# Loading a 256-element vector as one row and turning it on TensorE, in a recurrence and mixture-of-experts kernel

## The chip, the cores and the metric

The kernel runs on one core of a Trainium2 chip. The metric is the device time of one execution, in microseconds (us). It was run three times before the change; the median of these three runs is the time that counts, and lower is better.

## The reference, cut to what matters

Two stages follow each other. The first is a gated recurrence over a sequence, for 4 sequences of 5056 steps and 256 channels:

```python
sig = 1.0 / (1.0 + np.exp(-f_logit))
f = lower_bound[None, None, :] + (1.0 - lower_bound[None, None, :]) * sig
i = 1.0 - f
for t in range(S):
    h = f[:, t] * h + i[:, t] * x[:, t]
    y[:, t] = h
```

The second takes y as 20224 tokens and is a soft mixture of experts: `logits = x @ phi` for 32 slots, a softmax over the tokens that gathers them into slots, two matmuls for each of 8 experts with a ReLU between them, and a softmax over the slots that spreads the result back to the tokens.

`lower_bound` is a vector of 256 floats, 1 KB. Since f = 1 - (1 - lower_bound) * sigmoid(-f_logit), the kernel needs of it only `omlb` = 1 - lower_bound and `nomlb` = lower_bound - 1. Both are needed with channels on partitions: partition p holds the channels 2p and 2p + 1.

## The kernel before, in words

**Units.** The sequence is cut into groups of 512 tokens, and a unit is one group of one of the 4 sequences: 40 units. `load` (L195) issues the loads of `f_logit` (tile `f_t`) and `x` (tile `x_t`) on SyncE's queue (SP). The first six units are loaded one by one, 512 KB for each tensor (L216); the long middle part goes in transfers of 1 MB (L202). Three pairs of units fit the load buffers, so a later load waits for a buffer to come free.

**What a unit passes through.** ScalarE (ACT) computes sigmoid(-f) into `s_t` (`gate`, L226). GpSimd (POOL) multiplies it with x into `u_t` (`enter`, L237; VectorE does it for unit 0, L233). TensorE (PE) turns both from tokens on partitions to channels on partitions (`s_to_channels` and `u_to_channels`, L252 and L258, into the PSUM tiles `sp` and `up`). ACT makes the decay `a` = 1 + `nomlb` * s out of `sp` (`decay`, L286 and L293). VectorE (DVE) runs the recurrence as a scan (L304). PE turns the result back (`to_tokens`, L317, into the tile `hp`, which has the only PSUM buffer with the tag `tp`), DVE or ACT copies it out (`keep_tokens`, L334), and the matmuls of the second stage follow (`logits` L348, `slots` L398). At L174 PE runs matmuls that only add zero, as fillers. The expert weights are loaded on POOL's queue late in the first stage (L130, L140); then come the expert matmuls, and last the output blocks: matmul at L704 and L754, scaling at L694, L759 and L765, and stores on SP's queue.

**The order of the work** is written out by hand (`tc.manual_schedule()`); every engine executes its instructions in the order in which they are issued in the program, and waits on the semaphores of what it needs.

**The start, which the change touches.** `make_identity` builds `ident_f` on POOL. L75 loads `lower_bound` on ACT's queue into `lb`, and L79 loads phi on POOL's queue. Then DVE sets some constants. After the `load` calls of the first six units (L454), `lb_constants` (L103) computes `omlb` (L104) and `nomlb` (L105) on DVE. `gate(0)`, `enter(0)`, `s_to_channels(0)` and `decay(0)` come next: the first reader of `nomlb` is ACT's decay at L293. `phi_constants` (L107) follows on POOL: it scales phi by `omlb` (L109). `omlb` is read once more, much later (L598, L599).

The lines that count:

```python
lb = consts.tile([P, DC], F32, name="lb")
nc.scalar.dma_start(out=lb, in_=lower_bound.rearrange("(p o) -> p o", o=DC))
...
for n in range(SINGLE):
    load(n, 1)
lb_constants()
gate(0, 1)
enter(0)
s_to_channels(0)
```

Of the kernel before, what the change touches and what calls it, by code (L numbers as in the profile page):

```python
# [9 lines left out]
F32 = mybir.dt.float32  # L10
# [8 lines left out]
def kernel(  # L19
# [10 lines left out]
    nc = tc.nc  # L30
    B, S, D = x.shape
# [4 lines left out]
    P = 128  # L36
    DC = D // P
    FC = F // P
    R = 4
# [27 lines left out]
    consts = ctx.enter_context(tc.tile_pool(name="consts", bufs=1))  # L67
    ident_f = consts.tile([P, P], F32, name="ident_f")
# [2 lines left out]

    rep = consts.tile([P, B, NS], F32, name="rep")

    lb = consts.tile([P, DC], F32, name="lb")
    nc.scalar.dma_start(out=lb, in_=lower_bound.rearrange("(p o) -> p o", o=DC))  # L75
    omlb = consts.tile([P, DC], F32, name="omlb")
    nomlb = consts.tile([P, DC], F32, name="nomlb")
    phi_f = consts.tile([P, DC, NS], F32, name="phi_f")
# [22 lines left out]
        nc.vector.memset(parity[ds(b * NS, NS), ds(b % 2, 1)], 1.0)  # L101

    def lb_constants():  # L103
        nc.vector.tensor_scalar(omlb, lb, -1.0, 1.0, ALU.mult, ALU.add)  # L104
        nc.vector.tensor_scalar(nomlb, lb, 1.0, -1.0, ALU.mult, ALU.add)  # L105

# [49 lines left out]
    with tc.tile_pool(name="sp2", bufs=3) as sp2, \  # L156
# [297 lines left out]
# [5 lines that stand above are left out]
# [368 lines left out]
```

## Time and profile before

| | |
|---|---|
| three runs | 200.14, 200.80, 200.83 us; median 200.8 us |
| span of the profiled execution | 198.1 us; its own device time is not listed, so what lies around the span is 2.0 to 2.7 us by these runs |
| busy share of the span | PE 77%, DVE 72%, ACT 70%, PE's weight loads 56%, POOL 52% |
| moved by DMA | 70.77 MB, mean 357 GB/s |
| SP's DMA queue (q1) | 11520 packets, 62.00 MB |
| ACT's DMA queue (q10) | 288 packets, 0.13 MB |
| load of `lb` | 1 KB, issued at 0.72 us, landed 4.3 us later |
| `omlb`, `nomlb` on DVE | 169 ns, 164 ns |

The profile is that of one execution. Times in it count from the start of the span. "Busy" is the time in which an engine executed instructions. The chain of work that ended last is followed back from the last instruction: at each step to what released it, or to the instruction before it on its engine. In the table of stretches, the columns are the stretch and its length, then for PE, PE's weight loads (PEld), DVE, ACT and POOL the busy time with the number of instructions, then the TensorE clock that was granted (1.00 is full speed), the mean busy share of the 16 DMA engines, and the rate at which they moved data. A DMA queue's line gives the number of packets, the MB, and the time of its packets as a share of the 16 engines' time.

### The profile page before, as it was taken

Reading aid. Unit: us, or ns where it says so; the run is one execution under the profiler, and the core shown is the slowest. Engines: PE = TensorE matmul, PEld = TensorE weight load, DVE = VectorE, ACT = ScalarE, POOL = GpSimd, SP = SyncE. Lnnn points to the kernel's source line nnn. Section 1 sums busy time; section 2 is a strip of 40 time slices with the busy share of each in tenths; the row PEclk is TensorE's granted clock in tenths of the full one; section 3 lists DMA queues with packets and bytes.
Section 4 is the critical chain, followed back from the end, with each engine's and each line's share of the span. In section 5 each row is a group of like instructions: output and inputs, shape, how many; then the busy total and the mean of one; then the engine's idle time right before and its main releaser. Section 6 shows DMA issues by size and latency. Waiting matters only on the chain.

```text
span 198.1 us, 3497 instructions
## 1 busy us (share of the span) xinstructions
PE 153.3 (77%) x1330; PEld 110.4 (56%) x1330; DVE 143.3 (72%) x164; ACT 138.7 (70%) x195; POOL 103.0 (52%) x78
## 2 busy tenths in 40 slices
PE   0587599987999989898997978999989999950000
PEld 0366478776776768676695856568953543310000
DVE  1669869999699999999989999523268878840000
ACT  2688677899889999999897595622069889980000
POOL 2489578774998688884969969290030000000000
PEclk9999759997999999999999999999995555555555
DMA  5999999999999999999999999999639999999995
GB/s 177 418 420 419 427 429 429 427 427 357 378 424 424 408 337 420 432 411 307 407 420 392 241 215 214 213 212 211 110 110 419 430 421 427 450 443 424 424 424 218
DMA packets 14448, 70.77 MB, mean 357 GB/s; under 512 B 1744, under 2 KB 3024, under 8 KB 10464
## 3 DMA queue, kind: packets, MB, share of 16 engines
q1 hardware_dynamic: 11520, 62.00, 75.5%
q0 software_dynamic: 2624, 8.42, 21.3%
q8 instruction: 10, 0.16, 0.3%
q10 hardware_dynamic: 288, 0.13, 0.2%
q14 instruction: 6, 0.05, 0.1%
HBM read 58.23 MB, written 20.71 MB: 399 GB/s over the span
## 4 chain that ended last, share of the span: by engine, by line
PE 32%; DMA 30%; DVE 18%; POOL 6%; issue 3%; ACT 1%; ACTq 0%; SPq 0%; POOLq 0%
DMA x_t<-in_x_dram 15%; DVE h L304 13%; PE op L754 12%; DMA w_t<-in_moe_w_dram 8%; DMA w_sb<-in_moe_w_dram 7%; POOL u_t L237 5%; PE hp L317 4%; PE up L258 4%; PE sp L252 3%; DVE ht L334 3%; PE op L704 2%; PE slot_ps L174 2%; PE lg L348 1%; PE slot_ps L398 1%; DVE ob L694 1%
## 5 line engine op out<-in xcount | busy, mean ns | idle before, releaser
L237 POOL TENSOR_TENSOR u_t<-s_t,x_t 128x1024 bf16<-128x1024 bf16 (+1 forms) x39 | 82.5, 2128 | 23.3 <-ACT s_t L226 13.9
L304 DVE TENSOR_TENSOR_SCAN h<-a,h,up 128x512 bf16<-128x512 f32 (+1 forms) x72 | 86.9, 1252 | 4.7 <-PE up L258 2.5
L226 ACT ACTIVATE s_t<-f_t 128x2048 bf16<-128x2048 f32 (+2 forms) x23 | 38.3, 1668 | 5.8 <-DMA f_t<-in_f_logit_dram 4.5
L317 PE MATMUL hp<-ident_f,h 128*128 128x128 f32 (+1 forms) x160 | 29.5, 309 | 7.3 <-DVE ht L334 6.0
L317 PEld LDWEIGHTS hp<-ident_f,h 128*128 128x128 f32 (+1 forms) x160 | 23.1, 208 | 15.3 <-DVE ht L334 9.6
L252 PE MATMUL sp<-ident_f,s_t 128*128 128x128 f32 x144 | 22.6, 303 | 10.1 <-ACT s_t L226 7.8
L286 ACT ACTIVATE a<-sp,nomlb 128x1024 f32<-128x1024 bf16 x24 | 25.4, 1114 | 0.8 <-PE sp L252 0.6
L252 PEld LDWEIGHTS sp<-ident_f,s_t 128*128 128x128 f32 x144 | 18.6, 158 | 11.8 <-issue 6.0
L754 PE MATMUL op<-slot_bd,etall 64*128 64x512 bf16 x62 | 24.4, 600 | 0.1
L765 ACT ACTIVATE oc<-op,rrow 128x256 f32<-128x256 f32 x60 | 22.8, 490 | 1.4 <-PE op L754 0.9
L759 DVE TENSOR_TENSOR oc<-op,rrow 128x1024 f32<-128x1024 f32 x16 | 19.3, 1223 | 4.6 <-PE op L754 4.5
L293 ACT ACTIVATE a<-sp,nomlb 128x512 f32<-128x512 bf16 (+2 forms) x22 | 17.9, 859 | 4.8 <-PE sp L252 4.4
L258 PE MATMUL up<-ident_f,u_t 64*128 64x64 f32 x192 | 17.6, 229 | 2.0 <-POOL u_t L237 1.9
L174 PE MATMUL slot_ps<-rep,ident 128*128 128x256 bf16 x122 | 17.7, 281 | 0.0
L258 PEld LDWEIGHTS up<-ident_f,u_t 64*128 64x128 f32 x192 | 13.9, 138 | 5.9 <-POOL u_t L237 2.4
L754 PEld LDWEIGHTS <-etall 64*128 64x128 bf16 x62 | 9.0, 153 | 14.2 <-issue 11.6
L334 ACT COPY ht<-hp 128x512 f32<-128x512 f32 (+1 forms) x18 | 10.4, 580 | 8.0 <-PE hp L317 7.9
L334 DVE COPY ht<-hp 128x512 f32<-128x512 f32 (+1 forms) x22 | 14.7, 668 | 0.8 <-PE hp L317 0.8
L174 PEld LDWEIGHTS <-ident 128*128 128x128 bf16 x126 | 11.4, 102 | 3.4 <-issue 1.3
L304 DVE TENSOR_TENSOR_SCAN h<-a,up 128x512 bf16<-128x512 f32 x8 | 9.3, 1209 | 2.5 <-ACT a L293 1.8
L252 PE MATMUL up<-ident_f,u_t 128*128 128x128 f32 x48 | 9.8, 337 | 0.6 <-POOL u_t L237 0.6
L348 PE MATMUL lg<-h,phi 128*32 128x512 bf16 (+1 forms) x80 | 10.0, 411 | 0.0
(105 smaller groups left out, 147.8 us busy)
## 6 DMA issues: line engine op xcount, KB each, us to landing
f_t<-in_f_logit_dram SPq DMA_DIRECT2D x12, 1024.0 KB, 12.3
x_t<-in_x_dram SPq DMA_DIRECT2D x12, 1024.0 KB, 11.4
out_dram<-oc SPq DMA_DIRECT2D x6, 2048.0 KB, 13.1
w_sb<-in_moe_w_dram POOLq DMA_DIRECT2D x14, 512.0 KB, 10.3
f_t<-in_f_logit_dram SPq DMA_DIRECT2D x12, 512.0 KB, 8.6
x_t<-in_x_dram SPq DMA_DIRECT2D x12, 512.0 KB, 9.4
out_dram<-oc SPq DMA_DIRECT2D x4, 896.0 KB, 6.1
out_dram<-ob SPq DMA_DIRECT2D x1, 2048.0 KB, 8.9
```

Source lines behind the costliest of these rows:

```text
L174: nc.tensor.matmul(slot_bank[:, 1, ds(0, rhs.shape[1])], ident, rhs, start=first and i < 2, stop=False, skip_group_check=True)
L226: nc.scalar.activation(s_t, f_t, ACT.Sigmoid, scale=-1.0)
L237: nc.gpsimd.tensor_tensor(uts[n][:, :r], s_t[:, :r], x_t[:, :r], ALU.mult)
L252: nc.tensor.transpose(ps[:, :, r], t[:, r], ident_f)
L258: nc.tensor.transpose(v[:, :, r], t(r)[k].bitcast(F32), ident_f[k, k])
L286: nc.scalar.activation(a, sp[:, :, :, :, o], ACT.Identity, scale=nomlb[:, ds(o, 1)], bias=1.0)
L304: nc.vector.tensor_tensor_scan(h[:, :T, o], decays[n // 2, o][:, n % 2, :T], up[:, :T, o], hs[number(g - 1, b)][:, ds(used(g - 1) - 1, 1), ...
L317: nc.tensor.transpose(hp[:n_p, r], hw[:, :n_p, r], ident_f)
L334: copy(hts[g][:n_p, b].rearrange("p r d -> p (r d)").bitcast(F32), hps.pop(n)[:n_p].rearrange("p r c -> p (r c)"))
L754: nc.tensor.matmul(op[:, i_r].rearrange("p u d -> p (u d)"), ew[:, :, r + i_r], slot_bd[ds(j * 2 * NS, 2 * NS)].rearrange("s u d -> s (u d)"),
L759: nc.vector.tensor_tensor(ob[:, :, ds(r, k)].rearrange("p u r d -> p r u d"), op[:, ds(0, k)], scale[:, ds(r, k)].unsqueeze(3).broadcast_t ...
L765: nc.scalar.activation(ob[:, u, r + i_r], op[:, i_r, u], ACT.Copy, scale=scale[:, r + i_r, ds(u, 1)])
```

## The change

The vector is loaded as one contiguous row of 256 floats on partition 0. In `lb_constants`, two TensorE transposes with a 1x1 identity then turn the even and the odd channels of that row into two columns on 128 partitions, in a PSUM tile that takes the buffer with the tag `tp`. `omlb` and `nomlb` are computed from this PSUM tile.

```diff
-    lb = consts.tile([P, DC], F32, name="lb")
-    nc.scalar.dma_start(out=lb, in_=lower_bound.rearrange("(p o) -> p o", o=DC))
+    lb_row = consts.tile([1, D], F32, name="lb_row")
+    nc.scalar.dma_start(out=lb_row, in_=lower_bound.unsqueeze(0))
...
     def lb_constants():
+        row = lb_row.rearrange("u (p o) -> u p o", o=DC)
+        lb_ps = ptp.tile([P, R, P], F32, name="lb_ps", tag="tp")
+        lb = lb_ps[:, 0, ds(0, DC)]
+        for o in range(DC):
+            nc.tensor.transpose(lb_ps[:, 0, ds(o, 1)], row[:, :, o], ident_f[ds(0, 1), ds(0, 1)])
         nc.vector.tensor_scalar(omlb, lb, -1.0, 1.0, ALU.mult, ALU.add)
         nc.vector.tensor_scalar(nomlb, lb, 1.0, -1.0, ALU.mult, ALU.add)
```

## The prediction

> **What bounds the kernel now.** I read the page first, then the chain of work that ended last in order of time, then the first microseconds: the timeline, the table of stretches, and the DMA queues stretch by stretch.
>
> From the page: the span, the slices of 4.95 us, and the chain's shares.
>
> ```profile
> span 198.1 us, 3497 instructions
> ...
> PEclk9999759997999999999999999999995555555555
> DMA  5999999999999999999999999999639999999995
> GB/s 177 418 420 419 427 429 429 427 427 357 378 424 424 408 337 420 432 411 307 407 420 392 241 215 214 213 212 211 110 110 419 430 421 427 450 443 424 424 424 218
> ...
> PE 32%; DMA 30%; DVE 18%; POOL 6%; issue 3%; ACT 1%; ACTq 0%; SPq 0%; POOLq 0%
> ```
>
> No engine bounds the whole; the bound changes from stage to stage. From the second to the ninth slice (5 to 45 us) the loads run flat out at 418 to 429 GB/s; after that the rate moves with the engines. So the first 40 us are paced by the loads. The chain, with start, length and what it is, says the same:
>
> ```profile
> 0.72 0.38 SPq L216
> 1.10 0.06 issue
> 1.16 4.89 DMA x_t<-in_x_dram
> 6.05 0.02 issue
> 6.06 10.30 DMA x_t<-in_x_dram
> ...
> 21.26 13.88 DMA x_t<-in_x_dram
> ...
> 39.96 0.04 issue
> 40.00 0.46 PE up L258 x4
> ```
>
> The chain starts with unit 0's x (issued 1.16, landed 6.05) and stays on x transfers, with two POOL multiplies between, until 35.14; POOL multiplies lead to 40 us, and PE and DVE follow. Whatever shifts the load stream shifts all of this.
>
> The load of `lb` itself is not on the chain. From the timeline (start, length, engine, line):
>
> ```profile
> 4.85 1.06 ACT L226 ACTIVATE s_t<-f_t 128x1024 bf16<-128x1024 f32 x1 [2.41 <-DMA f_t<-in_f_logit_dram]
> 5.02 0.17 DVE L104 TENSOR_SCALAR omlb<-lb 128x2 f32<-128x2 f32 x1 [2.99 <-DMA lb<-in_lower_bound_dram]
> 5.10 0.16 DVE L105 TENSOR_SCALAR nomlb<-lb 128x2 f32<-128x2 f32 x1
> 7.17 0.69 ACT L293 ACTIVATE a<-sp,nomlb 128x512 f32<-128x512 bf16 x1 [1.27 <-PE sp L252]
> ```
>
> `nomlb` is ready at 5.26; its first reader starts at 7.17, and waits for PE. As a latency, `lb` has 1.9 us to spare. But the first slice moves only 177 GB/s. The table of stretches of half a microsecond shows where:
>
> ```profile
> 2.00:2.50 0.50, 0.00 (x0) 0.00 (x0) 0.04 (x2) 0.44 (x1) 0.31 (x1) 1.00 0.26 90
> 3.00:3.50 0.50, 0.00 (x0) 0.00 (x0) 0.00 (x0) 0.00 (x0) 0.00 (x0) 1.00 0.83 213
> 4.00:4.50 0.50, 0.00 (x0) 0.00 (x0) 0.00 (x0) 0.00 (x0) 0.00 (x0) 1.00 1.05 402
> 4.50:5.00 0.50, 0.00 (x0) 0.00 (x0) 0.00 (x0) 0.15 (x1) 0.00 (x0) 1.00 1.05 434
> ```
>
> and the DMA queues between 3.0 and 3.5 us:
>
> ```profile
> q1 hardware_dynamic: 26, 0.11, 80.0%
> q10 hardware_dynamic: 25, 0.00, 2.6%
> ```
>
> q10 is `lb`'s queue: 128 packets of 8 bytes and 16 of 4. For every 4 KB packet of the loads one small packet of `lb` goes through. From 4.5 us none is left, and the rate is full at once: 434 GB/s.
>
> **The change, part by part.**
>
> *128 small packets leave the stream (the only large term).* Six stretches from 1.5 to 4.5 us moved 115, 90, 271, 213, 279 and 402 GB/s: times 0.5 us, 685 KB. The first data move at about 1.7 us; 2.8 us at the 420 GB/s of the stretch from 6 to 10 us are 1176 KB. Missing are 491 KB, or 491/420 = 1.17 us. That is the upper end: all of it is due to `lb`. The lower end is 0: the stream starts slowly by itself, and no row of this trace shows a start without `lb`. I go near the upper end, because the shortage ends in the very stretch in which the small packets end, and because the two queues alternate one to one before that (33 and 18 packets in 2.5 to 3.0 us, 26 and 25, 36 and 38, 63 and 54), as if a small packet had to be done before the next large one began. The row still has packets: one for the data and one for the semaphore, or 16 and 16. Pro rata of 144 packets that leaves 2/144 to 32/144 of 1.17 us, 0.02 to 0.26 us. The gain is then 0.91 to 1.15 us; I take **1.0 us**.
>
> A rule of the Trainium skill speaks against this. DMA: Bandwidth & Descriptors, section "Why small descriptors are slow (HBM only)", puts a small packet's loss at a fixed handful of cycles on the engine's internal bus, plus 32 bytes of metadata. The row for 4.0 to 4.5 us seems to agree, since 54 small packets pass beside 402 GB/s, and q10 fills only 0.4% of the first 20 us, 0.08 us an engine. By the rule the change would be worth, as an estimate, less than 0.1 us, and the sum would be 200.7; the thin stretches from 2.0 to 4.0 us speak against it, and the run will decide.
>
> *What the 1.0 us becomes.* `f_t` and `x_t` of unit 0 land 1.0 us sooner (4.85 to 3.9, 6.05 to 5.05), and so does each transfer behind them, for the queue never runs dry. ACT's table load ended at 2.44, so the first sigmoid can start at 3.9. POOL is late next: phi lands on its own queue, the scaling of phi ends at 7.97, and unit 1's multiply (8.96, waiting for x) could now start at 7.9; the 0.1 us lost is made good in the next units, where POOL needs 2.15 us against 2.5 of the loads. The loads then pace the work to 40 us as before, and what follows starts from there: 1.0 us reaches the end unless the clock interferes (rivals).
>
> *The load on ACT's queue.* Its issue took 0.41 us (0.72 to 1.13). The next on ACT's queue is the table load, and ACT then idles 2.41 us for `f_t`. Cost and gain 0. When does the row land? `lb`'s packets ran from 2.1 to 4.5 us and it landed at 5.0, half a microsecond after the last. With at most 2 packets an engine instead of 9 I put the landing at 3.4; the late bound is 5.0, as now.
>
> *SP's queue.* In the waits of SP's own queue one issue (x of unit 3, at 5.01) waited 0.8 us for `lb`'s landing. With the row landing at 3.4 it follows its predecessor at 4.2. Five transfers are queued ahead of it then, so 0 gained.
>
> *Two transposes on PE.* None with one partition is in the trace. The nearest row is four 128x128 transposes at L252 in 1.08 us, 0.27 each; the lower bound is 0 each. Two cost 0 to 0.54 us; I take 0.5. They wait for `ident_f` (ready at 2.39) and the row. Queued behind them on PE are the transposes of unit 0's s, for which ACT's decay and DVE's first scan wait; these could start at 6.02 - 1.0 = 5.0. Row at 3.4 + 0.5 = 3.9: 1.1 us of cover, cost 0. With the row at 5.0 they end at 5.5 and hold PE up by 0.5 us; x, which sets the chain, lands at 5.05 and its transposes come only after DVE's multiply, so at most 0.5 us is at risk.
>
> *omlb and nomlb from PSUM.* Now 0.17 and 0.16 us; the nearest row that reads PSUM is L598, 128x32, 0.25 us. They cost 0 to 0.2 us more, end near 4.5 and are read after 6.1: 0.
>
> *The PSUM buffer.* The first `hp` in the same buffer is written by PE at 13.3 us. It now waits for `nomlb`, done 8 us earlier: 0.
>
> Sum: 198.1 - 1.0 = 197.1 us of span. What lies around the span is 2.0 to 2.7 us by the three runs; against their median, with 2.7, that is **199.8 us**.
>
> **The rivals.**
>
> 1. *The slow start is the stream's own, or the row's packets hold it up as much.* For it: the 16 DMA engines are only 30 to 40% busy from 1.6 to 2.0 us, before any small packet, and the rate at 4.0 to 4.5 is nearly full beside 54 of them. Against it: the one-to-one alternation. Gain 0 to 0.3 us: 200.5 to 200.8. This is also the case in which the change does not do what it says.
>
> 2. *Slower: one more half-clock window in the stage that PE paces.* The granted clock was 0.50 from 46.65 to 50.07 us, after a stretch (43.20 to 46.65) with PE busy for only 2.21 of 3.45 us. On the chain inside it, four transposes of L317 took 0.85 us against 0.48 outside, eight of L252 1.24 against 0.87, and six fillers 1.39 against 0.65 for five: 1.5 us lost in one window. If starting 1 us earlier puts another thin stretch whole into a window (70.0 to 73.4 and 92.0 to 95.4 had PE busy for 2.48 of 3.4 us, just above), 1.5 us are lost, 3 if the window is twice as long, as from 22.8 to 29.6. [...] Time: 200.8 - 1.0 + 1.5 = 201.3 to 202.8; with rival 1's gain, 202.0. It decides where the loss exceeds the gain.
>
> 3. *The reverse:* the window at 46.65 disappears as well, -1.0 - 1.5: 198.3.
>
> **How the numbers follow.** Forecast 0.64 (199.8, with 0.35 us to either side for how runs scatter, as the three did over 0.69 us), rival 1 0.19, rival 2 0.12, rival 3 0.05. About 0.5%, 1.0 us, is what a measurement of this kernel can tell from no change, and the forecast lies on that line: I give it 0.37 beyond and 0.27 within; rival 3 adds 0.05 to faster, rival 1 goes to no change but for 0.01 on the slower side, rival 2 splits, 0.09 slower and 0.03 within. Faster 0.42, same 0.48, slower 0.10. The range leaves out rival 3 and most of rival 2: 199.1 to 201.1.
>
> **What would show it.** In the profile after: q10 with at most 32 packets in the first 20 us; above 350 GB/s in the stretches from 2.0 to 4.0 us; the first sigmoid near 3.9 and the first scan near 7.3 instead of 8.29; two small PE instructions before 4.5; every later landing about 1.0 us earlier, with the same distance at 40 us and, if the clock windows agree, at the end. The prediction is wrong if the stretches stay at 90 to 280 GB/s without the small packets; if the landings come earlier but the distance is lost before 40 us, the loads did not pace that stage; if it is lost later with an additional 0.50 in the clock, it was rival 2.

## The result and the profile after

The changed kernel is slower. Its median over 22 runs is 201.21 us (200.85 to 202.25), that of the kernel before in the same runs 200.72 us (199.91 to 201.87); the ratio is 1.0043, 95% interval [1.0029, 1.0057]. The forecast was 199.8, the range 199.1 to 201.1.

The page of the changed kernel, the lines that answer to those shown of before:

```profile
span 199.3 us, 3501 instructions
...
PEclk9999759996999999999999999999985555555555
...
GB/s 212 413 409 410 419 418 419 421 416 345 396 423 416 395 340 419 421 406 303 403 408 360 268 226 216 214 213 213 119 107 402 416 413 441 437 421 421 421 421 263
...
q10 hardware_dynamic: 146, 0.13, 0.2%
```

The first slice went up from 177 to 212 GB/s: the loads start sooner. But the next eight are lower than before in every slice: 413 against 418, 409 against 420, 410 against 419, and so on, 1 to 3%. The stores at the end stand at 421 against 424. The clock has the same half-speed slices as before, so it is not what moved.

The start did about half of what was forecast. Timeline of the changed kernel (start, length, engine, line):

```profile
2.45 0.39 PE L108 MATMUL lb_ps<-ident_f,lb_row 1*128 1x1 f32 x2 [2.45 <-POOL ident_f masks.py:199]
2.88 0.16 DVE L109 TENSOR_SCALAR omlb<-lb_ps 128x2 f32<-128x2 f32 x1 [0.23 <-PE lb_ps L108]
4.29 1.06 ACT L231 ACTIVATE s_t<-f_t 128x1024 bf16<-128x1024 f32 x1 [1.73 <-DMA f_t<-in_f_logit_dram]
7.84 2.34 DVE L309 TENSOR_TENSOR_SCAN h<-a,up 128x512 bf16<-128x512 f32 x2 [0.85 <-PE up L257]
```

The row is there before 2.45 us, for the transposes wait for the identity and not for it; `omlb` is ready at 3.04 us, 1.2 us before the first sigmoid. That sigmoid starts at 4.29 instead of 4.85, and the first scan at 7.84 instead of 8.29. The stretches of half a microsecond (the last three columns are the granted clock, the DMA share, GB/s):

```profile
2.00:2.50 0.50, 0.05 (x1) 0.06 (x1) 0.11 (x3) 0.50 (x1) 0.31 (x1) 1.00 0.00 0
2.50:3.00 0.50, 0.34 (x2) 0.25 (x2) 0.27 (x3) 0.06 (x1) 0.00 (x0) 1.00 0.84 344
3.00:3.50 0.50, 0.00 (x0) 0.00 (x0) 0.10 (x2) 0.00 (x0) 0.00 (x0) 1.00 1.04 426
4.00:4.50 0.50, 0.00 (x0) 0.00 (x0) 0.00 (x0) 0.21 (x1) 0.00 (x0) 1.00 0.99 410
```

The stream is at full rate from 3.0 us and not from 4.0. Between 2.0 and 2.5 no packet starts all the same, with no small packet left: the first 4 KB packets of the loads, begun at 1.7 us, are still under way and take up to 985 ns each. That is a first sign that the slow start is not all due to `lb`.

**Where the lead went in these two profiles.** The last scan starts at 124.67 us in the kernel before and at 124.35 in the changed one: the engines keep 0.3 us of lead through the whole first stage. The chains show where it is lost. The end of the chain, kernel before:

```profile
113.81 14.12 DMA w_sb<-in_moe_w_dram
127.93 0.28 issue
128.21 15.66 DMA w_t<-in_moe_w_dram
143.88 0.04 issue
143.92 0.38 PE so_ps L664 x4
```

and the changed kernel:

```profile
113.50 15.19 DMA w_sb<-in_moe_w_dram
128.69 0.28 issue
128.98 15.63 DMA w_t<-in_moe_w_dram
144.60 0.04 issue
144.65 0.38 PE so_ps L669 x4
```

The expert weights are issued 0.31 us earlier, and land 0.76 us later (128.69 against 127.93). They share the DMA engines with the loads of x and f, which had fallen behind (their last packet ends at 117.28 us instead of 114.44); the last expert matmuls wait for them. From 0.32 us ahead to 0.73 behind, 1.05 us are lost there; another 0.48 go in the output stage, for the span is 1.21 us longer. Where the fall in the rate comes from is seen by counting packets. SP's DMA queue from 12 to 20 us, where it has the engines to itself (packets, MB, their time as a share of 16 engines), kernel before:

```profile
q1 hardware_dynamic: 919, 3.36, 102.7%
```

and the changed kernel:

```profile
q1 hardware_dynamic: 897, 3.28, 102.8%
```

The engines are equally full, but get through 897 packets instead of 919: each takes longer. In the packet records of these 8 us a 4 KB packet takes 159.0 ns before and 163.1 ns after. From 180 us on, 16 KB packets of the stores take 611.0 and 615.7 ns. Nothing in the diff names these transfers.

### The profile page after: what moved, and what is told of

Same layout as the page of the kernel before. It is cut to its first block, busy times and chain, and to the rows that moved or that the text cites. A ratio compares the mean times of both kernels' runs of the same rounds, so it can differ in the third digit from the quotient of the medians.

```text
span 199.3 us, 3501 instructions
## 1 busy us (share of the span) xinstructions
PE 154.8 (78%) x1332; PEld 110.5 (55%) x1332; DVE 143.3 (72%) x164; ACT 138.3 (69%) x195; POOL 103.2 (52%) x78
## 4 chain that ended last, share of the span: by engine, by line
PE 30%; DMA 30%; DVE 17%; POOL 8%; issue 3%; ACT 1%; SPq 0%; ACTq 0%; POOLq 0%
DMA x_t<-in_x_dram 15%; DVE h L309 12%; PE op L759 12%; DMA w_t<-in_moe_w_dram 8%; DMA w_sb<-in_moe_w_dram 8%; POOL u_t L242 6%; PE up L263 4%; PE hp L322 4%; PE sp L257 3%; DVE ht L339 3%; PE op L709 2%; PE slot_ps L179 2%; ACT oc L770 1%; PE lg L353 1%; PE slot_ps L403 1%
## 5 line engine op out<-in xcount | busy, mean ns | idle before, releaser
L759 PE MATMUL op<-slot_bd,etall 64*128 64x512 bf16 x62 | 24.9, 622 | 0.3 <-ACT oc L770 0.2
```

Source lines behind the costliest of these rows:

```text
L759: nc.tensor.matmul(op[:, i_r].rearrange("p u d -> p (u d)"), ew[:, :, r + i_r], slot_bd[ds(j * 2 * NS, 2 * NS)].rearrange("s u d -> s (u d)"),
```

## The experiments

Two theories were formed from the above: **A**, that the small packets had spread the 16 engines in a way that suits the stream, and **B**, that the rate of that one execution was accidental and the loss elsewhere. All twelve kernels have one table at the end of this section.

**before_again**, the kernel before, unchanged.

> The kernel before, once more, for a second profile of it. What is to be explained: in the profile of the changed kernel the loads start 0.55 us earlier, but then move at 410 GB/s from 6 to 12 us where the kernel before moved 419, so that the lead is lost later. Theory A (the start sets the rate: the 16 DMA engines keep the order in which they began, and the 128 small packets spread them out): 4 KB packets of 6 to 12 us again at 159 ns on average and 419 GB/s, span near 198.1. Theory B (the lower rate was the condition of the chip in that one execution, and the change costs its 0.4% elsewhere): the rate varies from profile to profile, so this one and the next cannot be told apart by it. Ratio 1.000 by either.

Measured: 159.0 ns, 420 GB/s from 6 to 12 us, span 198.1, ratio 1.0028 [1.0004, 1.0052]. One kernel against itself is off by 0.3% here (200.68 against 200.23 us); below, a difference of that size is read only where the packet times speak for it.

**after_again**, the changed kernel, unchanged.

> The changed kernel, once more, on the same chip as the run above. Theory A: 4 KB packets again at 163 ns, 410 GB/s from 6 to 12 us, expert weights landed about 1 us later than before, span near 199.3, ratio 1.004. Theory B: the rate of 6 to 12 us is that of the kernel before in this call to within 2 GB/s, and the ratio is still 1.003 to 1.006, with the lost time at a place that does not wait for a transfer.

Measured: 163.0 ns and 407 GB/s from 6 to 12 us, span 200.1, ratio 1.0055 [1.0034, 1.0075]. From 12 to 20 us the packet times of both kernels repeat to 0.1 ns (159.0 and 163.1). That ends theory B: the slower packets belong to the program. The times alone would not have shown it: 201.10 us stands 0.2% above the 200.68 of before_again.

The path of the loss is another one here. The loads end at 112.62 us, no load of weights is on the end of the chain, and the last scan starts at 126.74 us (before_again: 124.16). The clock was at half speed in three windows before 60 us (from 24.4, 34.6 and 48.3), in before_again in one (from 45.6). The clock in 40 slices, before_again and then after_again:

```profile
PEclk9999999996999999999999999999995555555555
PEclk9999979698899999999999999999995555555555
```

So the late weights are the path of the first pair of profiles, and how much of the loss other executions take through the clock is not settled. What is common to all of them is the longer packet.

**row_and_runs**, the change plus the old load.

```diff
     nc.scalar.dma_start(out=lb_row, in_=lower_bound.unsqueeze(0))
+    lb_runs = consts.tile([P, DC], F32, name="lb_runs")
+    nc.scalar.dma_start(out=lb_runs, in_=lower_bound.rearrange("(p o) -> p o", o=DC))
```

> The changed kernel with the 128 runs of 8 bytes loaded as well, right behind the row on the same queue, into a tile that nothing reads. Theory A: the small packets spread the starts of the engines as before, the loads move at 419 GB/s again, and the time returns to that of the kernel before, ratio 0.998 to 1.001. Theory B: the packets only cost their place in the stream (up to 0.6 us of a later start), ratio 1.004 to 1.007, as slow as the change or slower.

Measured: 159.0 ns and 419 GB/s from 12 to 20 us, span 198.1, ratio 0.9975 [0.9957, 0.9993]. It agrees with A, and yet A is wrong, as row_pad32 shows: the edit changed two things, a load and the 32 bytes that its tile takes.

**runs_and_turn**, the kernel before plus two transposes on PE.

```diff
     def lb_constants():
+        turn = ptp.tile([P, R, P], F32, name="turn", tag="tp")
+        for o in range(DC):
+            nc.tensor.transpose(turn[:, 0, ds(o, 1)], ident_f[ds(0, 1)], ident_f[ds(0, 1), ds(0, 1)])
```

> The kernel before with two transposes of one partition added on PE at the place where the change has them (of a row of the identity matrix, read by nobody); the 128 runs stay. It tells what the PE part and its PSUM buffer cost. Theory A: ratio 1.000 within 0.2%. Theory B, if the loss sits in the order on PE or in the clock windows: up to 1.004.

Measured: 159.0 ns, ratio 1.0012 [0.9984, 1.0041]. No cost of the PE part or of its PSUM buffer is seen.

What speaks against A is the stores: 16 KB packets take 611 ns in all kernels with the runs and 616 without, 140 us after the start and behind 30 us in which SP's queue moves nothing. So something had to differ that lasts. **Theory C:** the place of the buffers. Each tile takes a multiple of 32 bytes of every partition. `lb` took 32, the row takes 1024 (of all partitions, though it fills one), and every buffer allocated later lies 992 bytes higher. In the compiled programs `f_t` begins at byte 88320 = 345 x 256 before and at 89312 = 348 x 256 + 224 after; weights, x and output buffers likewise. The engines' work on moved buffers did not get longer: a multiply of POOL on 128x1024 took 2153 ns before and 2155 after, a sigmoid of 128x2048 1909 and a scan of 128x512 1267 in both.

**row_pad32**, the change with 32 bytes of padding behind the row (`f_t` at 89344 = 349 x 256).

```diff
+    consts.tile([P, 8], F32, name="pad")
     omlb = consts.tile([P, DC], F32, name="omlb")
```

> The first call fell out so: 4 KB packets took 159.0 ns in every kernel that loads the 128 runs and 163.0 ns in the changed one, in the stores at the end too (16 KB: 611 against 616 ns), where nothing of the start is left. A new theory, C: the row takes 1024 bytes of each partition where the runs took 32, so every later buffer lies 992 bytes higher. The load and store buffers began at a multiple of 256 bytes before (f_t at 88320 = 345 x 256); now they begin 224 bytes past one (89312). This kernel is the changed one with 32 bytes of padding behind the row: f_t at 89344 = 349 x 256. C: 159 ns, 419 GB/s from 6 to 12 us, with the early start kept: ratio 0.994 to 0.998, faster than both kernels. A (the small packets spread the engines): still 163 ns, ratio 1.004.

Measured: 159.0 ns, 420 GB/s from 12 to 20 us, median 199.42 us, ratio 0.9956 [0.9935, 0.9977]. The queue from 12 to 20 us is again that of the kernel before:

```profile
q1 hardware_dynamic: 918, 3.36, 102.7%
```

The page of this kernel has the rate back in both stages, with the early start kept:

```profile
GB/s 206 419 415 423 431 419 428 431 424 333 408 424 423 391 351 424 428 405 306 413 416 380 248 215 215 214 213 211 107 118 426 421 421 444 447 431 424 424 424 215
```

A fell: no small packets, and 159 ns. This version beats both kernels. The fastest executions say the same as the medians: 198.94 us, and 199.02 in its repetition below, against 200.85 and 200.91 of the changed kernel.

**runs_pad992**, the kernel before with 992 bytes of padding behind `lb`, so that every later buffer lies as in the changed kernel.

```diff
+    consts.tile([P, 248], F32, name="pad")
     omlb = consts.tile([P, DC], F32, name="omlb")
```

> The kernel before with 992 bytes of padding behind lb, so that every later buffer lies where the changed kernel has it (f_t at 89312, 224 bytes past a multiple of 256); the 128 runs stay, and nothing is done on PE. C: 163 ns and 410 GB/s, with the late start of the runs: span near 199.5 to 200.5, ratio 1.004 to 1.009. A: 159 ns, ratio 1.000.

Measured: 163.1 ns from 12 to 20 us, span 200.8, median 201.84 us, ratio 1.0086 [1.0062, 1.0110]. The placement alone, without any of the change's work, makes the kernel before slower than the change did. Its queue from 12 to 20 us:

```profile
q1 hardware_dynamic: 898, 3.28, 102.8%
```

**runs_pad64** and **runs_pad128**, the same with `[P, 16]` and `[P, 32]` as padding.

> The kernel before with 64 bytes of padding: f_t at 88384, a multiple of 64 but 64 past a multiple of 256. If a buffer must start at a multiple of 64 only, 159 ns and ratio 1.000; if at a multiple of 256, longer packets (160 to 164 ns) and ratio 1.001 to 1.006. A: 159 ns.

> The kernel before with 128 bytes of padding: f_t at 88448, 128 past a multiple of 256. By the page DMA: Bandwidth & Descriptors of the Trainium skill, section on how a descriptor splits into AXI transactions, each packet that does not start at a multiple of 256 is split once more. If the split is what costs, about as slow as the run with 64 bytes: 160 to 164 ns. If only the 32-byte remainder costs: 159 ns, ratio 1.000.

Measured: 163.0 and 163.1 ns, ratios 1.0129 [1.0086, 1.0172] and 1.0072 [1.0042, 1.0101]. A multiple of 64 or of 128 isn't enough; of the placements tried only a multiple of 256 has the short packets, and 64, 128 and 224 bytes past it cost the same to 0.1 ns. The larger ratio of the first is not all placement: its profile has a half-clock window from 144.5 to 148.0 us that the others lack.

The Trainium skill, DMA: Bandwidth & Descriptors, section "How a descriptor splits into AXI transactions", says that a transfer is cut into pieces of 256 bytes, each of which must start at a multiple of 256, so that a start off such a multiple fetches, and pays for, the bytes ahead of it. It does not say that the written side, which is the SBUF side of a load, is meant too. This case agrees that it costs; in size it doesn't. Counted in the page's 32-byte beats, 4 KB would take 130, 132 and 135 beats for 64, 128 and 224 bytes instead of 128, which as an estimate makes 161.5, 164.0 and 167.7 ns out of 159; measured is 163 for all three.

**row_pad32_again**, **row_loads_at_256**, **row_stores_at_256**: which buffers matter. In the second the 32 bytes stand behind the weights, so that only the load buffers and what follows lie at a multiple of 256; in the third 32 bytes stand in front and 224 more behind the weights, so that weights and output buffers do.

```diff
# row_loads_at_256: the change, with
     w2_sb = [wts.tile([P, FC, D], BF16, name=f"w2_sb{e}") for e in range(E - 2)]
+    wts.tile([P, 8], F32, name="pad_w")
# row_stores_at_256: row_pad32, with
+    wts.tile([P, 56], F32, name="pad_w")
```

> The changed kernel with 32 bytes of padding once more, as the yardstick of this call and for a second measurement of the gain. C: packets of 159 ns again, ratio 0.994 to 0.998.

> The changed kernel with the 32 bytes of padding put between the expert weights and the load buffers: f_t and x_t begin at a multiple of 256 (89344), the weights and the output buffers 224 past one (31968). It tells what the stores and weights cost. C: 4 KB packets of the loads 159 ns, 16 KB packets of the stores 616 instead of 611 ns: 0.8% of the 49 us of the output stage, 0.4 us more than the yardstick, ratio 0.996 to 1.000.

> The other way round: weights and output buffers at a multiple of 256 (32000), the load buffers 224 past one (89568). It tells what the loads cost. C: loads 163 ns, 410 GB/s, stores 611 ns. The two parts should add up to the 1.7 us between the changed kernel and the padded one: 1.0 to 1.4 us more than the yardstick, ratio 1.000 to 1.004.

Measured: medians 199.42, 199.82 and 200.90 us. Off the multiple the stores cost 0.40 us, the loads 1.48, together 1.88; the changed kernel stood 1.68 above row_pad32 (201.10 against 199.42, in different series of runs). The parts add up within what the runs scatter. The part of the stores is no larger than that scatter, and rests on the packets: 611.0 ns in row_pad32_again, 615.4 with the stores off the multiple. From 12 to 20 us, row_loads_at_256:

```profile
12.00:20.00 8.00, 7.36 (x40) 6.63 (x40) 7.93 (x8) 6.67 (x9) 7.36 (x6) 1.00 1.03 420
```

and row_stores_at_256:

```profile
12.00:20.00 8.00, 6.90 (x40) 6.01 (x40) 7.97 (x9) 6.64 (x9) 7.23 (x6) 1.00 1.03 410
```

Its weights land late on the chain as they do in the changed kernel:

```profile
113.61 15.20 DMA w_sb<-in_moe_w_dram
129.09 15.64 DMA w_t<-in_moe_w_dram
```

**no_load_pad32**, row_pad32 with the row set to 0.5 instead of loaded.

```diff
-    nc.scalar.dma_start(out=lb_row, in_=lower_bound.unsqueeze(0))
+    nc.vector.memset(lb_row, 0.5)
```

> The padded kernel without the load of lower_bound: the row is set to 0.5 by VectorE (so the output is that of another lower_bound). It tells how fast the stream starts with nothing of lower_bound in it. Prediction on record: a clean start, the first f_t landed before 3.9 us. Rival 1 on record, the slow start is the own start of the stream: landing near 4.3 us as with the row, first 4 KB packets still several hundred ns long, ratio as the yardstick within 0.1%.

Measured: median 199.37 us, span 197.6; first `f_t` landed at 4.50 us. Its stretches:

```profile
2.00:2.50 0.50, 0.06 (x1) 0.06 (x1) 0.29 (x5) 0.00 (x1) 0.31 (x1) 1.00 0.22 49
2.50:3.00 0.50, 0.34 (x2) 0.25 (x2) 0.28 (x3) 0.00 (x0) 0.00 (x0) 1.00 0.61 221
3.00:3.50 0.50, 0.00 (x0) 0.00 (x0) 0.10 (x2) 0.00 (x0) 0.00 (x0) 1.00 1.04 426
```

With nothing of `lower_bound` in the stream it still crawls until 3 us. Rival 1 of the prediction held for the larger part: most of the slow start is the stream's own. The load of the row costs nothing that these runs can see.

| kernel | start of f_t past a multiple of 256 | 4 KB packet, 12 to 20 us | median, us | ratio, 95% interval |
|---|---|---|---|---|
| before_again | 0 | 159.0 ns | 200.68 | 1.0028 [1.0004, 1.0052] |
| runs_and_turn | 0 | 159.0 ns | 200.67 | 1.0012 [0.9984, 1.0041] |
| row_and_runs | 0 | 159.0 ns | 199.86 | 0.9975 [0.9957, 0.9993] |
| row_pad32 | 0 | 159.0 ns | 199.42 | 0.9956 [0.9935, 0.9977] |
| row_pad32_again | 0 | 159.0 ns | 199.42 | 0.9943 [0.9922, 0.9965] |
| no_load_pad32 | 0 | 159.0 ns | 199.37 | 0.9934 [0.9903, 0.9965] |
| row_loads_at_256 | 0, stores 224 | 159.0 ns | 199.82 | 0.9967 [0.9942, 0.9992] |
| row_stores_at_256 | 224, stores 0 | 163.1 ns | 200.90 | 1.0027 [1.0001, 1.0053] |
| after_again | 224 | 163.1 ns | 201.10 | 1.0055 [1.0034, 1.0075] |
| runs_pad992 | 224 | 163.1 ns | 201.84 | 1.0086 [1.0062, 1.0110] |
| runs_pad64 | 64 | 163.0 ns | 203.10 | 1.0129 [1.0086, 1.0172] |
| runs_pad128 | 128 | 163.1 ns | 201.35 | 1.0072 [1.0042, 1.0101] |

## Why the prediction was wrong

- **What failed** is the step "What the 1.0 us becomes", with its premise that every later transfer only moves in time. The prediction followed the row's instructions, queues and waits, and never what its tile takes of SBUF. The 992 bytes moved every buffer off a multiple of 256, each 4 KB packet of the load stream took 163.1 ns instead of 159.0, and the placement cost 1.6 to 1.7 us of the whole (201.84 against 200.23, 201.10 against 199.42), more than the start gained. That is shown both ways: padding the change by 32 bytes takes it away, padding the kernel before by 992 bytes brings it in. None of the three rivals had it; rival 2 put the slower case on the clock, whose half-speed windows lay alike in the two main profiles (from 22.8 and 46.7 us before, from 22.1 and 46.0 after). In after_again there were more of them, so the clock may add to the loss in some executions; but from 12 to 20 us the packets are longer while the clock is full (1.00).
- **The one large term was mis-sized.** 1.0 us was to be gained by the clean start, of 1.17 that the prediction counted as missing from 1.7 to 4.5 us. By the same sum 0.75 us are still missing in the changed kernel (862 of 1176 KB moved), and 0.91 in no_load_pad32 (795 KB), where nothing of `lower_bound` is loaded. The first sigmoid came 0.56 us sooner and the first scan 0.45 in the two main profiles. Over all profiles the first `f_t` is taken up at 4.46 to 4.85 us in the six with the runs alone (mean 4.68), and at 4.28 to 4.68 in the six with the row alone (mean 4.40): 0.3 us. The first scan says the same, 8.16 to 8.31 (mean 8.25) against 7.83 to 8.17 (mean 7.91). The lower end of the range, that the stream starts slowly by itself, was the better guess, and the one-to-one alternation of packets was not evidence of a price: without any small packet the stream is as thin until 2.5 us. The prediction's estimate of less than 0.1 us, from the low price of a small packet in the Trainium skill, DMA: Bandwidth & Descriptors, section "Why small descriptors are slow (HBM only)", was nearer than 1.0 but looks too low.
- **What lies around the span** was 1.8 us and not 2.0 to 2.7: 1.76 to 1.80 on average in every kernel whose runs list both. An execution with a span of 198.1 us takes 199.9 (before_again), so the profile before the change was of a fast execution. The forecast is not moved by it, for it comes to the median less 1.0.
- **ACT's queue, SP's queue:** right in effect. The row's issue took 0.52 us instead of 0.41, before an idle stretch; it landed before 2.45 us, sooner than the 3.4 put down. The wait of SP for `lb` is gone and gained nothing to be seen.
- **PE:** right. Two transposes took 0.39 us together against the 0.5 taken, and ended 2.5 us before the transposes of s were due.
- **omlb, nomlb, the PSUM buffer:** right, 0.16 and 0.15 us, read later than they are made.
- **The lead reaching 40 us and beyond:** on the engines it nearly did in the main pair of profiles, 0.3 us at the last scan. But the prediction looked for the end on the engines' chain, and the weights, which come through the same 16 DMA engines after the loads, were late.

**What stays open.** The padded change is 0.4 to 0.6% below the kernel before, 0.8 to 1.0 us. That is close to the 1.0 us of the forecast, but it does not bear the forecast out, for only 0.3 us of it is seen at the start. The two profiles understate the difference (197.7 against 198.1 us of span): over all runs the median span is 197.65 us with the padding, and 198.5 and 198.7 before. One comparison with equal placement bears on the small packets alone: row_and_runs has `f_t` at 89344, as row_pad32 has, and differs from it by the load of the runs. Its first scan starts at 8.41 us instead of 7.88, and its median is 199.86 against 199.42, in different series of runs. The 0.37 us that are left between row_and_runs and the kernel before (200.23) are no more than that kernel differed from itself. Part of the difference may also be the clock: the two profiles of before had two and one half-clock windows in the first 60 us, the padded ones one each. No run here settled it. Why an offset of 64, 128 or 224 bytes costs the same wasn't settled either.

## What to carry to other kernels

A constant that grows moves every buffer allocated after it, so note the start address of the big transfer buffers before and after an edit, and pad them back to the multiple they had (here 256 bytes). When a change that touches 1 KB shifts the time of the whole kernel, compare the duration of one packet or one instruction of the same shape far away from it; a difference there that repeats belongs to the program. And an experiment that adds a buffer changes the layout as well, so take one whose padding alone is changed beside it.

## What the runs showed of the hardware

- A packet to or from an SBUF buffer that starts 64, 128 or 224 bytes past a multiple of 256 took 163.0 to 163.1 ns instead of 159.0 (4 KB loads), 314 to 315 instead of 309 (8 KB loads, 30 to 40 us), 615 to 616 instead of 611 (16 KB stores): about 4 to 6 ns a packet whatever its size, so small packets lose the larger share. The packets of POOL's queue that load and convert the weights were not touched: 322 to 325 ns either way.
- The row went out as one packet of 1 KB and one of 4 bytes, the runs as 128 of 8 bytes and 16 of 4.
- The stream of loads needs until about 3 us to come to its full rate with nothing else in it; its first 4 KB packets took up to 985 ns in the changed kernel, and up to 1272 in no_load_pad32.
